# Feed-forward blocks of two groups, skewed accumulator drains and triangular diagonal scores in a gated-attention kernel

## The chip, the cores and the metric

The kernel runs on one core of one Trainium2 chip. The metric is the device time of one execution in microseconds; medians of several executions are given. The profiles show the TensorE clock granted in full (0.995 or more). A profile's span is 2 to 3 us shorter than the time of its execution. Names: PE is TensorE (matmuls), PEld its weight loads, DVE is VectorE, ACT is ScalarE, POOL is GpSimd, SP is SyncE, whose queue issues most DMAs here.

## The reference

```python
# u, v: (8, 3072, 256); z: (8, 3072, 64); w1, w2: (256, 1024); w_out: (1024, 256)
scores = (1 / S) * z @ z.T            # per batch, symmetric: 3072 x 3072
attn   = maximum(scores, 0) ** 2
x      = u * (attn @ v)               # 24576 rows of 256
out    = maximum(x @ w1, x @ w2) @ w_out
```

## The kernel before

A batch has 24 tiles of 128 rows, in 6 groups (512 query columns each), so there are 48 groups in all. For each group the kernel multiplies 24 tiles of attention by v (64-row matmuls, two at a time: rows 0 to 63 and 64 to 127 of the array work on their own halves of the contraction and sum into accumulators of their own). Since the attention matrix is symmetric, a block above the diagonal is computed once and its mirror image is made by a DMA transpose. Scores are computed up to 11 pairs of tiles ahead. After each group, the feed-forward of the group before it runs with 128-row matmuls, while ACT and DVE add up the two halves of the accumulators ("drain"). max(h1, h2) is computed as relu(x (w1 - w2)) + x w2, with w2 @ w_out folded once.

```python
def score_pair(b, g, m, ...):            # two tiles of scores; diagonal blocks in full
    for h in range(2):
        rows = ds(h * R, R)              # R = 64: one half of the array each
        nc.tensor.matmul(s_ps[h], zT[b][rows, 2 * m + h, :], zT[b][rows, ds(g * G, G), :]...)
    for h in range(2):
        nc.scalar.activation(r[:, h, :], s_ps[h], AF.Relu)
    nc.vector.tensor_mul(a[:, k : k + 2, :], r, r)
    ...                                  # mirror(b, g, blk): a DMA transpose on SP

def attn_unit(b, g, t, acc, first, last):
    for dc in range(KD):                 # two halves of d (128 columns each)
        for half in range(2):            # two halves of the array
            nc.tensor.matmul(acc[half][:, dc, :], v_sb[b][rows, t, ts(dc, P)], a..., ...)

def drain(acc):                          # both d halves at once, after the last tile
    for dc in range(KD):
        nc.scalar.copy(h, acc[1][:, dc, :])
    for dc in range(KD):
        nc.vector.tensor_add(hs[dc], hs[dc], acc[0][:, dc, :])

for i, (b, g) in enumerate(groups):
    for n in range(NT):                  # 24 tiles
        ahead(...)                       # at 8 of the tiles one more pair of scores
        attn_unit(b, g, n, acc, n == 0, n == NT - 1)
        if i and n == 12:
            waiting.append((*groups[i - 1], gate(*groups[i - 1], sums)))
        ...                              # loads, mirrors, z of the next batch in group 3
    now = waiting if i >= 2 else []      # one group per block (two at i = 2)
    g_sbs = [ff(w) for w in now[:1]]
    sums = drain(acc)
    ...                                  # ff2 of each; stores
```

## Time and profile before

The time before is 977.95 us (977.77 to 978.25). The page of the profiled execution gives for each engine the busy time, its share of the span and the number of instructions.

```profile
span 975.8 us, 19097 instructions
PE 962.4 (99%) x7994; PEld 516.8 (53%) x8042; DVE 495.4 (51%) x752; ACT 580.3 (59%) x1058; POOL 61.0 (6%) x118
PE 98%; DVE 1%; issue 0%; ACT 0%
```

The third line is the chain of work that ended last, by engine. PE is the bound in nearly the whole span. The view of the waits has for PE, the three largest first: engine, line and what it wanted, whom it waited for, then us in total, how often, and the longest.

```profile
PE acc_431 L184 <- DVE h_sb L195: 1.8, 1, 1.8
PE acc_644 L184 <- DVE h_sb L195: 1.8, 1, 1.8
PE s_ps L136 <- DVE r_sb L147: 1.5, 3, 0.7
```

These are the hand-overs of the accumulators after groups 0 and 1, where no feed-forward hides the drain, and waits for scores in the start; what is left out is 2.0 us in all, also of the start. The timeline of PE has the start, how long it took, the instruction and its count. Matmuls are pipelined, so what one costs is the time from its start to the next start.

```profile
202.21 0.38 PE L184 MATMUL acc_2591<-a_sb,v_sb 64*128 64x512 bf16 x1
202.22 0.38 PE L184 MATMUL acc_2592<-a_sb,v_sb 64*128 64x512 bf16 x1
202.43 0.38 PE L184 MATMUL acc_2591<-a_sb,v_sb 64*128 64x512 bf16 x1
202.43 0.38 PE L184 MATMUL acc_2592<-a_sb,v_sb 64*128 64x512 bf16 x1
202.74 3.63 PE L215 MATMUL d_ps<-xT,w_sb 128*128 128x512 bf16 x15
209.70 1.04 PE L244 MATMUL o_ps<-w_out_sb,g_sb 128*128 128x256 bf16 x8
210.67 0.39 PE L136 MATMUL s_ps<-zT 64*128 64x512 bf16 x2
210.90 0.38 PE L184 MATMUL acc_2859<-at_sb,v_sb 64*128 64x512 bf16 x1
```

A pair of 64-row matmuls takes 0.215 us (202.21 to 202.43). From the last such pair to the first 128-row matmul it is 0.31 us, so the switch costs 0.09 us; back again it costs the same.

| What | read from | value |
|---|---|---|
| pair of 64-row matmuls, 512 columns | timeline | 0.215 us |
| o_ps matmul, 256 columns | starts in the trace | 0.109 us |
| last attention pair to first d_ps | timeline | 0.31 us |
| last o_ps to first s_ps | starts in the trace | 0.205 us |
| feed-forward blocks | timeline | 46 |

### The profile page before, as it was taken

The page shows a single profiled execution, that of the slowest core. Times are in us where ns is not written, and L with a number is a line of the kernel's source. Part 1 is how long each engine was busy: PE and PEld are TensorE (multiplying, and loading weights), DVE is VectorE, ACT ScalarE, POOL GpSimd, SP SyncE. Part 2 cuts the span into 40 slices and gives each one's busy share as a digit, 9 for nine tenths or more (in the row PEclk, how much of TensorE's full clock was granted, in tenths as well). Part 3 has the DMA queues.
Part 4 walks back from the last instruction along what each step waited for, and adds up shares of the span by engine and source line. Part 5 has one row for each costly group of instructions (what it writes and reads, how often), then busy time and mean ns, then how long its engine had stood idle before and what let it go on. Part 6 is the DMA issues. An engine that isn't in the chain of part 4 may idle for free.

```text
span 975.8 us, 19097 instructions
## 1 busy us (share of the span) xinstructions
PE 962.4 (99%) x7994; PEld 516.8 (53%) x8042; DVE 495.4 (51%) x752; ACT 580.3 (59%) x1058; POOL 61.0 (6%) x118
## 2 busy tenths in 40 slices
PE   8899999999999999999999999999999999999998
PEld 3465555555555555555555555555555555555555
DVE  6645455554545544555445653555535564455523
ACT  7756466664666646666466664666546665466623
POOL 3101001000000000000000000000000000000000
PEclk9999999999999999999999999999999999999999
DMA  9999758786598866898668974789657896576411
GB/s 183 176 220 192 146 113 164 158 149 129 114 176 150 152 122 118 162 167 146 107 144 154 170 140 99 150 162 166 127 109 153 155 163 123 123 134 136 91 55 44
DMA packets 346005, 137.69 MB, mean 141 GB/s; under 512 B 324544, under 2 KB 325696, under 8 KB 345920
## 3 DMA queue, kind: packets, MB, share of 16 engines
q1 hardware_dynamic: 329504, 106.98, 54.9%
q0 software_dynamic: 16416, 29.50, 19.4%
q8 instruction: 63, 1.03, 0.4%
q14 instruction: 22, 0.18, 0.1%
HBM read 59.77 MB, written 25.17 MB: 87 GB/s over the span
## 4 chain that ended last, share of the span: by engine, by line
PE 98%; DVE 1%; issue 0%; ACT 0%
PE d_ps L215 17%; PE o_ps L244 17%; PE s_ps L136 8%; PE o_ps L236 4%; PE acc_12285 L184 1%; PE acc_12095 L184 1%; PE acc_10820 L184 1%; PE acc_10564 L184 1%; PE acc_10296 L184 1%; PE acc_10028 L184 1%; PE acc_9764 L184 1%; PE acc_9023 L184 1%; PE acc_8223 L184 1%; PE acc_7959 L184 1%; PE acc_1573 L184 1%; PE acc_11833 L184 1%
## 5 line engine op out<-in xcount | busy, mean ns | idle before, releaser
L151 ACT ACTIVATE r_sb<-s_ps 128x512 bf16<-128x512 f32 x663 | 360.4, 596 | 147.4 <-PE s_ps L136 147.3
L155 DVE TENSOR_TENSOR a_sb<-r_sb 128x1024 bf16<-128x1024 bf16 x335 | 231.5, 692 | 370.1 <-ACT r_sb L151 369.0
L184 PEld LDWEIGHTS <-v_sb 64*128 64x128 bf16 x4608 | 225.5, 94 | 270.7 <-issue 3.9
L244 PE MATMUL o_ps<-w_out_sb,g_sb 128*128 128x256 bf16 x1536 | 199.0, 273 | 0.0
L225 DVE TENSOR_SCALAR g_sb<-d_ps 128x512 bf16<-128x512 f32 x192 | 132.8, 692 | 95.9 <-PE d_ps L215 95.9
L223 ACT ACTIVATE g_sb<-d_ps 128x512 bf16<-128x512 f32 x192 | 114.6, 597 | 110.0 <-PE d_ps L215 109.9
L215 PE MATMUL d_ps<-xT,w_sb 128*128 128x512 bf16 x720 | 171.4, 380 | 2.5
L244 PEld LDWEIGHTS <-g_sb 128*128 128x128 bf16 x1536 | 150.2, 98 | 20.8
L251 ACT COPY o_sb<-o_ps 128x512 f32<-128x512 f32 x96 | 56.2, 585 | 129.1 <-PE o_ps L244 128.0
L136 PE MATMUL s_ps<-zT 64*128 64x512 bf16 x672 | 129.2, 377 | 2.3 <-DVE r_sb L147 1.5
L215 PEld LDWEIGHTS <-w_sb 128*128 128x128 bf16 x768 | 71.4, 98 | 98.5 <-issue 19.1
L113 POOL DMA_DIRECT2D un<-in_u_dram x48 | 25.6, 533 | 819.4 <-DMA uT<-un 798.2
L236 PE MATMUL o_ps<-W2o_sb,xT 128*128 128x256 bf16 x384 | 73.3, 273 | 0.0
L201 DVE SCALAR_TENSOR_TENSOR xT<-h_sb,uT 128x512 bf16<-128x512 f32 x96 | 61.7, 684 | 0.0
L136 PEld LDWEIGHTS <-zT 64*128 64x128 bf16 x672 | 33.1, 94 | 45.9 <-issue 10.0
L236 PEld LDWEIGHTS <-xT 128*128 128x128 bf16 x384 | 37.6, 98 | 14.1
L109 POOL DMA_DIRECT2D v_sb<-in_v_dram x48 | 25.9, 551 | 1.0 <-POOLq L426 0.8
L184 PE MATMUL acc_135<-a_sb,v_sb 64*128 64x512 bf16 x48 | 12.5, 376 | 0.0
L184 PE MATMUL acc_134<-a_sb,v_sb 64*128 64x512 bf16 x48 | 12.5, 376 | 0.0
L184 PE MATMUL acc_1795<-a_sb,v_sb 64*128 64x512 bf16 x48 | 11.6, 376 | 0.0
L184 PE MATMUL acc_3336<-a_sb,v_sb 64*128 64x512 bf16 x48 | 11.6, 376 | 0.0
L184 PE MATMUL acc_7960<-a_sb,v_sb 64*128 64x512 bf16 x48 | 11.6, 376 | 0.0
(302 smaller groups left out, 1213.5 us busy)
## 6 DMA issues: line engine op xcount, KB each, us to landing
out_dram<-o_sb SPq DMA_DIRECT2D x47, 512.0 KB, 3.0
v_sb<-in_v_dram POOLq DMA_DIRECT2D x48, 256.0 KB, 7.0
un<-in_u_dram POOLq DMA_DIRECT2D x48, 256.0 KB, 4.8
zn<-in_z_dram POOLq DMA_DIRECT2D x7, 384.0 KB, 6.2
at_sb<-a_sb SPq DMA_TRANSPOSE x120, 4.4
uT<-un SPq DMA_TRANSPOSE x48, 3.6
w_132<-in_moe_w_dram POOLq DMA_DIRECT2D x1, 512.0 KB, 5.2
w_131<-in_moe_w_dram POOLq DMA_DIRECT2D x1, 512.0 KB, 7.4
```

Source lines behind the costliest of these rows:

```text
L109: nc.gpsimd.dma_start(out=v_sb[b][:, sl, :], in_=by_tile(v[b])[:, sl, :])
L136: nc.tensor.matmul(s_ps[h], zT[b][rows, 2 * m + h, :], zT[b][rows, ds(g * G, G), :].rearrange("p t c -> p (t c)"), start=True, stop=True,)
L151: nc.scalar.activation(r[:, h, :], s_ps[h], AF.Relu)
L155: nc.vector.tensor_mul(a[:, k : k + 2, :], r, r)
L184: nc.tensor.matmul(o, v_sb[b][rows, t, ts(dc, P)], mv, start=first, stop=last)
L201: nc.vector.scalar_tensor_tensor(out=xT[:, dc, :].rearrange("p (t r) -> p t r", r=P), in0=hs[dc].rearrange("p (t r) -> p t r", r=P), scala ...
L215: nc.tensor.matmul(d_ps, w15_sb[:, kc, ts(nb, P)], xT[:, kc, :], start=(kc == 0), stop=(kc == KD - 1),)
L223: nc.scalar.activation(g_sb[:, nb, :], d_ps, AF.Relu)
L225: nc.vector.tensor_single_scalar(out=g_sb[:, nb, :], in_=d_ps, scalar=0.0, op=ALU.max)
L236: nc.tensor.matmul(o_ps[:, t, :], xT[:, dc, ts(t0 + t, P)], W2o_sb[:, dc, :], start=(dc == 0), stop=False,)
L244: nc.tensor.matmul(o_ps[:, t, :], g_sb[:, nb, ts(t0 + t, P)], w_out_sb[:, nb, :], start=False, stop=(nb == KF - 1),)
L251: nc.scalar.copy(o_sb[:, t0 : t0 + 2, :], o_ps)
```

## The change

The intent is to give PE fewer and shorter slots. (1) A feed-forward block follows every second group only and does two groups, so PE switches between 64-row and 128-row matmuls less often. (2) After the groups without a block the accumulators are handed over without a gap: in the last 9 tiles (4 in groups 0 and 1) the matmuls of the first d half all come before those of the second, and the next group begins the same way, so that one half drains while the other is computed; in groups 0 and 1 the drain is two plain copies, added later. (3) From batch 1 on, a diagonal block computes only its upper triangle, and three small DMA transposes fill in the rest; its tiles come last in the group. (4) The start has fewer score pairs ahead, and the prefetches in batch 0 are held back by a small DVE write before them.

```diff
+        triangle = blk == g and whole_first < (b, g)
+        lo = [(k + h) * P if triangle else 0 for h in range(2)]
         for h in range(2):
             rows = ds(h * R, R)
             nc.tensor.matmul(
-                s_ps[h],
+                s_ps[h][:, lo[h] :],
                 zT[b][rows, 2 * m + h, :],
-                zT[b][rows, ds(g * G, G), :].rearrange("p t c -> p (t c)"),
+                zT[b][rows, g * G + lo[h] // P : g * G + G, :].rearrange("p t c -> p (t c)"),
 ...
+        if triangle and m % 2 == 1:
+            for j in range(G - 1):
+                nc.sync.dma_start_transpose(
+                    a[:, j + 1 :, ts(j, P)], a[:, j, (j + 1) * P :]
+                )
 ...
+    def drain_fast(acc, dc):
+        hs = [hpool.tile([P, GW], fp32, name="h_sb") for half in range(2)]
+        nc.scalar.copy(hs[1], acc[1, dc])
+        nc.vector.tensor_copy(hs[0], acc[0, dc])
 ...
+    def ff_follows(i):
+        return i >= 2 and i % 2 == 0 or i == len(groups) - 1
+    def edge(i):
+        return 0 if ff_follows(i) else 4 if i < 2 else 9
+    def steps_of(i):
+        head = edge(i - 1) if i else 0
+        tail = NT - edge(i)
+        steps = [(n, dc) for dc in both for n in tiles[:head]]
+        steps += [(n, dc) for n in tiles[head:tail] for dc in both]
+        return steps + [(n, dc) for dc in both for n in tiles[tail:]]
+    def pair_slots(i):
 ...
+        if ff_follows(i):
+            return [3, 9, 15, 21, 26, 31, 36, 40]
+        return [0, 5, 10, 15, 20, 25, 30, 41]
 ...
+                if n == NT - 1 and not ff_follows(i):
+                    if i < 2:
+                        new[dc] = drain_fast(acc, dc)
+                    else:
+                        new.update(drain(acc, [dc]))
 ...
+                if i in (1, 2) and n == 10:
+                    for h in sums.values():
+                        nc.vector.tensor_add(h[0], h[0], h[1])
 ...
-            now = waiting if i >= 2 else []
+            now = waiting if ff_follows(i) else []
```

Cut from the diff: buffer counts (uT 4 to 3, h_sb 2 to 4, xT 3 to 4), the order of tiles, the triangular relus and squares, the held prefetches, the start.

More of the change, by code (lines that the diff above doesn't have):

```diff
@@ L49 @@
     unat = ctx.enter_context(tc.tile_pool(name="unat", bufs=2))
-    upool = ctx.enter_context(tc.tile_pool(name="upool", bufs=4))
+    upool = ctx.enter_context(tc.tile_pool(name="upool", bufs=3))
     apool = ctx.enter_context(tc.tile_pool(name="apool", bufs=11))
@@ L53 @@
     rpool = ctx.enter_context(tc.tile_pool(name="rpool", bufs=3))
-    hpool = ctx.enter_context(tc.tile_pool(name="hpool", bufs=2))
-    xpool = ctx.enter_context(tc.tile_pool(name="xpool", bufs=3))
+    hpool = ctx.enter_context(tc.tile_pool(name="hpool", bufs=4))
+    xpool = ctx.enter_context(tc.tile_pool(name="xpool", bufs=4))
     gpool = ctx.enter_context(tc.tile_pool(name="gpool", bufs=2))
@@ L65, with load_z @@
     zn, zd, zT, v_sb, un, uT = {}, {}, {}, {}, {}, {}
-    def load_z(b, lo, n):
+    def load_z(b, lo, n, held=False):
         if b not in zn:
@@ L72, in load_z @@
         sl = ds(lo, n)
+        if held:
+            nc.vector.memset(zn[b][:, lo, 0:1], 0.0)
         nc.gpsimd.dma_start(out=zn[b][:, sl, :], in_=by_tile(z[b])[:, sl, :])
@@ L103, in zT_pe, with load_v @@
         copy(zT[b][:, lo : lo + n, :], tp)
-    def load_v(b, lo, n):
+    def load_v(b, lo, n, held=False):
         if b not in v_sb:
@@ L108, in load_v @@
         sl = ds(lo, n)
+        if held:
+            nc.vector.memset(v_sb[b][:, lo, 0:1], 0.0)
         nc.gpsimd.dma_start(out=v_sb[b][:, sl, :], in_=by_tile(v[b])[:, sl, :])
@@ L124 @@
     later = []
+    whole_first = (0, NG - 1)
+    V_ORDER = (1, 2, 3, 4, 5, 0)
     V_LATE = [(3, 14), (4, 8), (4, 14), (5, 2), (5, 8), (5, 14)]
@@ L131, in score_pair @@
         a = A[b, g, blk]
+        k = 2 * (m % 2)
+        triangle = blk == g and whole_first < (b, g)
+        lo = [(k + h) * P if triangle else 0 for h in range(2)]
         s_ps = []
@@ L143, in score_pair @@
         r = rpool.tile([P, 2, GW], bf16, name="r_sb")
-        k = 2 * (m % 2)
         for h in range(2):
+            s, o = s_ps[h][:, lo[h] :], r[:, h, lo[h] :]
             if h == dve_half:
-                nc.vector.tensor_single_scalar(
-                    out=r[:, h, :], in_=s_ps[h], scalar=0.0, op=ALU.max
-                )
-            else:
-                nc.scalar.activation(r[:, h, :], s_ps[h], AF.Relu)
-            if halves:
-                nc.vector.tensor_mul(a[:, k + h, :], r[:, h, :], r[:, h, :])
-        if not halves:
-            nc.vector.tensor_mul(a[:, k : k + 2, :], r, r)
+                nc.vector.tensor_single_scalar(out=o, in_=s, scalar=0.0, op=ALU.max)
+            else:
+                nc.scalar.activation(o, s, AF.Relu)
+        if halves or triangle:
+            for h in range(2):
+                o = r[:, h, lo[h] :]
+                nc.vector.tensor_mul(a[:, k + h, lo[h] :], o, o)
+        else:
+            nc.vector.tensor_mul(a[:, k : k + 2, :], r, r)
+        if triangle and m % 2 == 1:
+            for j in range(G - 1):
+                nc.sync.dma_start_transpose(
+                    a[:, j + 1 :, ts(j, P)], a[:, j, (j + 1) * P :]
+                )
         if m % 2 == 1 and blk > g:
@@ L169, in mirror, with attn_unit, drain @@
         A[b, blk, g] = t
-    def attn_unit(b, g, t, acc, first, last):
+    def attn_unit(b, g, t, acc, dc, first, last):
         blk, j = divmod(t, G)
         a = A[b, g, blk]
-        for dc in range(KD):
-            for half in range(2):
-                rows = ds(half * R, R)
-                if blk >= g:
-                    o, mv = acc[half][:, dc, :], a[rows, j, :]
-                else:
-                    o = acc[half][:, dc, :].rearrange("p (k r) -> p k r", r=P)
-                    mv = a[rows, :, j, :]
-                nc.tensor.matmul(
-                    o, v_sb[b][rows, t, ts(dc, P)], mv, start=first, stop=last
-                )
-    def drain(acc):
-        hs = []
-        for dc in range(KD):
-            h = hpool.tile([P, GW], fp32, name="h_sb")
-            nc.scalar.copy(h, acc[1][:, dc, :])
-            hs.append(h)
-        for dc in range(KD):
-            nc.vector.tensor_add(hs[dc], hs[dc], acc[0][:, dc, :])
+        for half in range(2):
+            rows = ds(half * R, R)
+            if blk >= g:
+                o, mv = acc[half, dc], a[rows, j, :]
+            else:
+                o = acc[half, dc].rearrange("p (k r) -> p k r", r=P)
+                mv = a[rows, :, j, :]
+            nc.tensor.matmul(o, v_sb[b][rows, t, ts(dc, P)], mv, start=first, stop=last)
+    def drain(acc, dcs):
+        hs = {}
+        for dc in dcs:
+            hs[dc] = hpool.tile([P, GW], fp32, name="h_sb")
+            nc.scalar.copy(hs[dc], acc[1, dc])
+        for dc in dcs:
+            nc.vector.tensor_add(hs[dc], hs[dc], acc[0, dc])
+        return hs
+    def drain_fast(acc, dc):
+        hs = [hpool.tile([P, GW], fp32, name="h_sb") for half in range(2)]
+        nc.scalar.copy(hs[1], acc[1, dc])
+        nc.vector.tensor_copy(hs[0], acc[0, dc])
         return hs
@@ L260, with tiles_of @@
     W2o_sb = consts.tile([P, KD, D], bf16)
+    def ff_follows(i):
[3 more added lines that the diff above has]
+    def steps_of(i):
+        tiles, both = range(NT), range(KD)
+        head = edge(i - 1) if i else 0
[4 more added lines that the diff above has]
+    def pair_slots(i):
+        if i == 0:
+            return [1, 3] + list(range(6, 40, 4))
+        if i == 1:
+            return list(range(3, 41, 4))
+        if ff_follows(i):
+            return [3, 9, 15, 21, 26, 31, 36, 40]
+        return [0, 5, 10, 15, 20, 25, 30, 41]
     groups = [(b, g) for b in range(B) for g in range(NG)]
+    def tiles_of(b, g):
+        own = list(range(g * G, g * G + G))
+        rest = list(range(g * G + G, NT))
+        return list(range(g * G)) + (own + rest if (b, g) <= whole_first else rest + own)
     pairs, need = [], {}
     for i, (b, g) in enumerate(groups):
-        for n in range(NT):
-            if n // G >= g and n % 2 == 0:
-                pairs.append((b, g, n // 2))
-            need[i, n] = len(pairs)
+        order = [(b, g, m) for m in range(2 * g, NT // 2)]
+        base = len(pairs)
+        pairs += order
+        most = base
+        for n, t in enumerate(tiles_of(b, g)):
+            if t // G >= g:
+                most = max(most, base + order.index((b, g, t // 2)) + 1)
+            need[i, n] = most
     done = 0
@@ L278, in ahead @@
                 *pairs[done],
-                dve_half=1 if early and (done % 3 == 0 or done < 2) else None,
+                dve_half=1 if early and done % 3 == 0 else None,
                 halves=done == 0,
@@ L306, in new_acc @@
         def new_acc():
-            return [
-                acc_psum.tile([P, KD, GW], fp32, name=f"acc{half}") for half in range(2)
-            ]
+            return {
+                (half, dc): acc_psum.tile([P, GW], fp32, name=f"acc{half}{dc}")
+                for half in range(2)
+                for dc in range(KD)
+            }
         first_acc = new_acc()
@@ L315, in keep_warm @@
                 nc.tensor.matmul(
-                    first_acc[0][:, 0, :w], warm[:, :P], warm[:, :w], start=True, stop=True
+                    first_acc[0, 0][:, :w], warm[:, :P], warm[:, :w], start=True, stop=True
                 )
@@ L328 @@
         ahead(1)
-        zT_pe(0, 4, 8, "act")
+        zT_pe(0, 4, 8, "dve")
         keep_warm([P] * 2)
@@ L332 @@
         keep_warm([P] * 4)
-        ahead(3)
         waiting, sums = [], None
@@ L337 @@
             acc = new_acc() if i else first_acc
-            for n in range(NT):
+            new, slots = {}, pair_slots(i)
+            for slot, (n, dc) in enumerate(steps_of(i)):
                 k = need[i, n]
-                if b == 0 and g < 2:
-                    ahead(max(k, done + 1) if n % 2 == 0 and n < 22 else k)
-                else:
-                    more = n in (0, 3, 6, 9, 12, 15, 18, 20)
-                    ahead(max(k, min(done + 1, k + AHEAD)) if more else k)
-                if i == 0 and n == 5:
-                    zT_pe(0, 12, 8, "act")
-                if i == 0 and n == 11:
-                    zT_pe(0, 20, 4, "act")
-                attn_unit(b, g, n, acc, n == 0, n == NT - 1)
+                ahead(max(k, min(done + 1, k + AHEAD)) if slot in slots else k)
+                if i == 0 and slot in (10, 22):
+                    zT_pe(0, 12 if slot == 10 else 20, 8 if slot == 10 else 4, "act")
+                attn_unit(b, g, tiles_of(b, g)[n], acc, dc, n == 0, n == NT - 1)
+                if n == NT - 1 and not ff_follows(i):
+                    if i < 2:
+                        new[dc] = drain_fast(acc, dc)
+                    else:
+                        new.update(drain(acc, [dc]))
+                if dc:
+                    continue
+                if i in (1, 2) and n == 10:
+                    for h in sums.values():
+                        nc.vector.tensor_add(h[0], h[0], h[1])
+                    sums = {k: h[0] for k, h in sums.items()}
                 if i and n == 12:
@@ L367 @@
                 if later and n % 4 == 0 and (i > 1 or i == 1 and n > 12):
+                    later.sort(key=lambda block: block[2])
                     mirror(*later.pop(0))
@@ L379 @@
                     late = int(b == 0)
-                    if (g, n) == (2, 10):
-                        load_z(b + 1, 0, NT)
+                    if (g, n) == (2, 10 if b else 20):
+                        load_z(b + 1, 0, NT, held=late)
                     if (g, n) == (3, 4):
@@ L385 @@
                     if g >= 3 and n in (8, 14) and not late:
-                        load_v(b + 1, (2 * (g - 3) + (n == 14)) * G, G)
+                        load_v(b + 1, V_ORDER[2 * (g - 3) + (n == 14)] * G, G)
                     if late and (g, n) in V_LATE:
-                        load_v(1, V_LATE.index((g, n)) * G, G)
+                        load_v(1, V_ORDER[V_LATE.index((g, n))] * G, G, held=True)
             if i == 2:
@@ L400 @@
                     nc.scalar.copy(W2o_sb[:, dc, :], ps)
-            now = waiting if i >= 2 else []
+            now = waiting if ff_follows(i) else []
             g_sbs = [ff(w) for w in now[:1]]
-            sums = drain(acc)
+            sums = new or drain(acc, range(KD))
             for j, w in enumerate(now):
```

## The prediction

> **What bounds the kernel now.** TensorE. The page has PE busy 962.4 of 975.8 us (99%), ACT 59%, DVE 51%; the chain that ended last is 98% PE; the waits view gives PE only 7.1 us of waits: twice 1.78 us where the first two groups hand over their accumulators (waiting for the additions into h_sb), 2.3 us for scores and zT in the start. Only fewer or shorter PE slots help. A pair of 64-row matmuls of 512 columns takes a slot of 0.2155 us (timeline).
>
> **What the change removes.**
> 1. Switches between 64-row and 128-row matmuls. From the last attention start to the first d_ps is 0.31 us (202.43 to 202.74) instead of 0.215; from the last o_ps to the first s_ps about 0.20 instead of 0.11: 0.095 us each way. The Trainium skill ("TensorEngine Tiling (Array Packing)", Key Properties) says that changing the tiling mode drains the TensorE; this agrees. There are 46 feed-forward blocks now and 24 after: 22 x 0.19 = 4.2 us.
> 2. Triangles, 42 diagonal blocks in batches 1 to 7. Score pairs shrink from 512+512 to 512+384 and 256+128 columns. The halves run side by side and start in order, so the longer counts: only the second pair gains half a slot (0.107 us): 4.5 us, say 4.2.
> 3. The two hand-overs of 1.78 us. The copies of one d half run on ACT and DVE together (0.6 us each), but four tiles hide only 0.9 us and DVE still has a square (0.69 us) in front: I expect 0.6 us left at each, 2.3 us saved.
> 4. The start: attention no longer waits for a third and fourth score pair: 0.4 us.
>
> **What it adds.**
> - At the 22 odd boundaries without a feed-forward the accumulators must drain under the other d half. From the trace: last matmul's start to end of drain is 0.41 + 0.6 (copy) + 0.67 (addition), about 1.75 us; nine tiles and a score pair give 2.37 us. No wait expected.
> - Scores run less far ahead. By my count of slots, in group 2 of each batch the last pair is computed 13 slots (2.8 us) before use, where score to square takes 2.25 us: just free. In batch 0 it is 9 to 12 slots (was 15 to 21), while DVE gets the delayed additions and the gating (1.3 us each): 1.5 us of new waits.
> - 126 small DMA transposes, a tenth more transposed blocks, on a queue with a 55% share, some 13 us before use: no effect.
>
> **Sum.** 4.2 + 4.2 + 2.3 + 0.4 - 1.5 = 9.6, about 10 us, 1.0%, all on the critical path.
>
> Predicted 968.0 us; eight times in ten between 963.5 and 972.5. Faster by over 2%: 0.02; within 2%: 0.95; slower by over 2%: 0.03.
>
> **What would show each step.** Timeline: feed-forward blocks of two groups, none after odd groups; s_ps pairs of 256 and 128 columns with 0.107 us to the next start. Waits: the two 1.78 us down to about 0.6; nothing at odd boundaries; no PE wait for a triangle's DMA; 1 to 2 us for a_sb in the first 60 us.
>
> **What would make it wrong.** PE waits at odd boundaries (0.3 us each would cost 7 us) because ACT or DVE drains late; a stall in group 2 of every batch for scores (1 us each: 7 us); the 384-column half saving too (2 us more); transposes landing late in batch 0, whose DMA is busiest.

## The result, and the profile after

The changed kernel takes 969.06 us (968.62 to 969.40, 4 runs) against 977.95 us; the ratio is 0.9908 (0.9891 to 0.9926). Ratios are the mean time of one kernel's runs over that of the other's of the same rounds, so not quite the ratio of the medians.

The lines of the page that answer to those of before:

```profile
span 966.4 us, 19478 instructions
PE 954.8 (99%) x7994; PEld 621.6 (64%) x8042; DVE 487.2 (50%) x847; ACT 557.6 (58%) x1058; POOL 61.0 (6%) x118
PE 96%; DVE 1%; issue 1%; ACT 1%; DMA 1%; DVEq 0%; POOLq 0%
```

PE is as full as before, with the same number of matmuls, in 9.4 us less. The largest of its waits (the first is the start's first memset, as before):

```profile
PE acc_134 L374 <- DVE warm L351: 1.2, 1, 1.2
PE acc_427 L199 <- DVE a_sb L166: 1.1, 3, 0.5
PE acc_427 L199 <- DVE h_sb L214: 0.5, 1, 0.5
PE s_ps L147 <- DVE r_sb L158: 0.5, 1, 0.5
PE acc_134 L199 <- DMA v_sb<-in_v_dram: 0.4, 1, 0.4
PE acc_637 L199 <- DVE a_sb L166: 0.4, 1, 0.4
```

The two hand-overs of 1.78 us have become one of 0.5. All these waits lie in the first 51 us: acc_427 is group 1, acc_637 group 2. No boundary after that has a wait for a drain. In exchange, PE now waits 1.5 us in groups 1 and 2 for squares of scores (a_sb) that DVE does late; waits for relus (r_sb) there were before too (1.5 us, now 0.5).

A count in the trace, from the start of the last o_ps of one block to the start of the first d_ps of the next, shows the steady state of a batch (batches 2 to 6, the same in every one; the rows one_ff, full_mm and swap_rows are experiments below). With one group per block the stretches are those of groups 0 to 5; with two, those of groups 1 and 2, 3 and 4, and 5 and the next batch's 0:

```
attention between blocks, us            sum   feed-forward blocks, us
before    12.40 12.40 12.40 12.40 12.18 11.32   73.10   6 x  7.72
one_ff    12.29 12.29 12.29 12.18 12.07 11.32   72.44   6 x  7.72
full_mm   24.48       24.48       23.19         72.15   3 x 15.54
after     24.37       24.16       23.08         71.61   3 x 15.54
swap_rows 24.32       24.00       23.03         71.35   3 x 15.54
```

The start of the first block (in the third group) came at 53.79 us instead of 55.17. These 1.4 us are not all gain: a count in the trace gives 31 pairs of score matmuls before that block where there were 33, and the two missing ones (0.43 us) are only done later. So 1.0 us of the gain lies in the start. The profile also shows something that I had not expected. PE's timeline after the change, around a triangle:

```profile
200.61 0.38 PE L199 MATMUL acc_2833<-at_sb,v_sb 64*128 64x512 bf16 x1
200.67 0.38 PE L199 MATMUL acc_2835<-at_sb,v_sb 64*128 64x512 bf16 x1
200.83 0.38 PE L199 MATMUL acc_2833<-at_sb,v_sb 64*128 64x512 bf16 x1
200.89 0.22 PE L147 MATMUL s_ps<-zT 64*128 64x128 bf16 x1
200.94 0.38 PE L199 MATMUL acc_2835<-at_sb,v_sb 64*128 64x512 bf16 x1
201.05 0.27 PE L147 MATMUL s_ps<-zT 64*128 64x256 bf16 x1
201.16 0.38 PE L199 MATMUL acc_2833<-at_sb,v_sb 64*128 64x512 bf16 x1
```

acc_2833 is summed by rows 0 to 63, acc_2835 by rows 64 to 127. In the program the 256-column matmul (rows 0 to 63) stands before the 128-column one (rows 64 to 127), and yet the latter starts 0.16 us earlier, and even the attention matmul behind it (200.94) is ahead. The two halves of the array run as two streams, and the second has got ahead by the columns that it was spared. What becomes of this lead shows at the end of the stretch, where the first d_ps of the next block begins:

```profile
211.74 0.38 PE L199 MATMUL acc_2836<-a_sb,v_sb 64*128 64x512 bf16 x1
211.84 0.38 PE L199 MATMUL acc_2833<-a_sb,v_sb 64*128 64x512 bf16 x1
212.06 0.38 PE L199 MATMUL acc_2834<-a_sb,v_sb 64*128 64x512 bf16 x1
212.36 0.39 PE L234 MATMUL d_ps<-xT,w_sb 128*128 128x512 bf16 x1
```

Rows 64 to 127 start their last matmul at 211.74 (acc_2836). Rows 0 to 63 still have two to do (211.84 and 212.06), and the block starts 0.31 us after the last of these, as it did before the change. After the block both halves start level again (228.34). The lead has bought nothing.

### The profile page after: what moved, and what is told of

The parts are those of the page before. It is cut to its first block, busy times and chain, and to the rows that moved or that the text cites. A ratio compares the mean times of both kernels' runs of the same rounds, so it can differ in the third digit from the quotient of the medians.

```text
span 966.4 us, 19478 instructions
## 1 busy us (share of the span) xinstructions
PE 954.8 (99%) x7994; PEld 621.6 (64%) x8042; DVE 487.2 (50%) x847; ACT 557.6 (58%) x1058; POOL 61.0 (6%) x118
## 4 chain that ended last, share of the span: by engine, by line
PE 96%; DVE 1%; issue 1%; ACT 1%; DMA 1%; DVEq 0%; POOLq 0%
PE o_ps L263 17%; PE d_ps L234 17%; PE s_ps L147 7%; PE o_ps L255 4%; DMA v_sb<-in_v_dram 1%; DVE a_sb L166 1%; PE acc_12604 L199 1%; PE acc_6354 L199 1%; PE acc_4771 L199 1%; PE acc_3187 L199 1%; PE acc_11103 L199 1%; PE acc_9519 L199 1%; PE acc_7936 L199 1%; PE acc_1582 L199 1%; PE acc_1581 L199 1%
## 5 line engine op out<-in xcount | busy, mean ns | idle before, releaser
L199 PEld LDWEIGHTS <-v_sb 64*128 64x128 bf16 x4608 | 314.6, 94 | 181.4 <-issue 5.9
L160 ACT ACTIVATE r_sb<-s_ps 128x512 bf16<-128x512 f32 (+3 forms) x664 | 333.8, 555 | 90.4 <-PE s_ps L147 88.8
L166 DVE TENSOR_TENSOR a_sb<-r_sb 128x1024 bf16<-128x1024 bf16 x251 | 173.6, 692 | 243.0 <-ACT r_sb L160 239.0
L234 PE MATMUL d_ps<-xT,w_sb 128*128 128x512 bf16 x720 | 167.4, 379 | 2.6 <-issue 0.2
L147 PE MATMUL s_ps<-zT 64*128 64x512 bf16 (+3 forms) x672 | 148.6, 357 | 0.9 <-DVE r_sb L158 0.5
L147 PEld LDWEIGHTS <-zT 64*128 64x128 bf16 x672 | 47.6, 94 | 29.0 <-issue 4.6
L164 DVE TENSOR_TENSOR a_sb<-r_sb 128x512 bf16<-128x512 bf16 (+3 forms) x170 | 47.9, 323 | 14.7 <-ACT r_sb L160 14.5
L199 PE MATMUL acc_134<-a_sb,v_sb 64*128 64x512 bf16 x24 | 8.7, 377 | 0.5 <-DMA v_sb<-in_v_dram 0.4
L199 PE MATMUL acc_136<-a_sb,v_sb 64*128 64x512 bf16 x24 | 8.7, 378 | 0.0
L199 PE MATMUL acc_137<-a_sb,v_sb 64*128 64x512 bf16 x24 | 8.5, 376 | 0.0
L199 PE MATMUL acc_135<-a_sb,v_sb 64*128 64x512 bf16 x24 | 8.5, 376 | 0.0
```

Source lines behind the costliest of these rows:

```text
L147: nc.tensor.matmul(s_ps[h][:, lo[h] :], zT[b][rows, 2 * m + h, :], zT[b][rows, g * G + lo[h] // P : g * G + G, :].rearrange("p t c -> p (t ...
L160: nc.scalar.activation(o, s, AF.Relu)
L164: nc.vector.tensor_mul(a[:, k + h, lo[h] :], o, o)
L199: nc.tensor.matmul(o, v_sb[b][rows, t, ts(dc, P)], mv, start=first, stop=last)
L234: nc.tensor.matmul(d_ps, w15_sb[:, kc, ts(nb, P)], xT[:, kc, :], start=(kc == 0), stop=(kc == KD - 1),)
```

## The experiments

Each kernel is the changed one with the edit shown. Those of one batch ran on the same chip, with the kernel before (978.0 us in each batch). The changed kernel itself ran only in the first batch (again, one_ff, full_mm, swap_rows); the others ran on another chip and are compared with its 968.96 us, as the kernel before took the same time on both.

### What the two main parts are worth

> The changed kernel unedited, so that the others of this batch have it beside them on the same chip: 969 us, PE waits of about 5 us in all, none of them at a boundary after the third group.

It took 968.96 us (968.32 to 969.18), and its trace had one wait that the first trace had not: 0.6 us for the transposed z of a batch. More of that below.

```diff
 def ff_follows(i):
-    return i >= 2 and i % 2 == 0 or i == len(groups) - 1
+    return i >= 2
```

> The changed kernel with a feed-forward block after every group again (46 blocks instead of 24, and no boundary without one). If the pair-wise blocks gain only by 22 fewer switches each way between 64-row and 128-row matmuls, at 0.19 us for both, the time rises by 4.1 us to 973.2. Rival: pairing the groups gains (or costs) something else, such as ACT and DVE evictions that no longer stand in the way of the drains; then the rise is not 4 us, and PE waits at the boundaries change.

It took 972.78 us (972.60 to 973.20), 3.8 us more than the changed kernel, and PE had no wait at any boundary after the second group. The switches account for it (22 x 0.188 = 4.1 by the gaps between starts; the changed kernel also loses 0.6 us that one_ff does not, see full_mm, so that without this loss the rise would be 4.4). The rival, that pairing gains through other engines, is not needed. The edit also removes the skew at these boundaries and moves their score pairs, since both follow ff_follows; PE has no wait there in either kernel.

```diff
             nc.tensor.matmul(
-                s_ps[h][:, lo[h] :],
+                s_ps[h],
                 zT[b][rows, 2 * m + h, :],
-                zT[b][rows, g * G + lo[h] // P : g * G + G, :]...
+                zT[b][rows, g * G : g * G + G, :]...
```

> The changed kernel with the diagonal blocks' score matmuls at all 512 columns again; the relus, the squares and the small transposes stay triangular. If the triangle gains through TensorE's slots alone, the time rises by 42 x 0.107 = 4.5 us to 973.5. Rival: it gains through less work on ACT and DVE; then the time stays at 969.

It took 972.70 us (971.80 to 972.97), 3.7 us more than the changed kernel, though ACT and DVE still did triangles: the gain is PE's slots. It is 0.8 us less than 42 x 0.107. The table says where: the stretches are 0.11, 0.32 and 0.11 us shorter than with full matmuls, which is five times 0.107 per batch and not six. The sixth is lost in group 2 of each batch. The timeline of the changed kernel there, first DVE, then PE:

```profile
286.04 1.28 DVE L220 SCALAR_TENSOR_TENSOR xT<-h_sb,uT 128x512 bf16<-128x512 f32 x2
287.25 0.68 DVE L166 TENSOR_TENSOR a_sb<-r_sb 128x1024 bf16<-128x1024 bf16 x1
287.63 0.42 PE L147 MATMUL s_ps<-zT 64*128 64x128 bf16 x2
287.98 0.37 PE L199 MATMUL acc_3863<-a_sb,v_sb 64*128 64x512 bf16 x1
```

DVE's gating (the multiplication by u, 1.28 us) stands before the square; the square ends at 287.93, and the attention matmul that needs it starts at 287.98. The 256-column slot in front of it lasted 0.198 us instead of 0.107, in this spot of each of the 7 batches, 0.6 us in all. So the supply of scores in group 2, which I had counted as "just free", is late by 0.1 us once the slots are shorter. That the gating is the cause is read from the order of times (ACT had finished the relus of this square at 286.70, DVE the gating at 287.33); I did not run a kernel with the gating moved. The trace of one_ff has no such slot: there all six triangles count (73.10 - 72.44 = 0.66 us per batch). The loss needs pairing and triangles together, and so both 3.8 and 3.7 us are what is left after it; each part alone is worth about 0.6 us more.

### Can the lead of one half be used?

```diff
         for h in range(2):
-            rows = ds(h * R, R)
+            rows = ds((1 - h if triangle and m % 2 else h) * R, R)
```

> The changed kernel, but in the second pair of a triangle the 256-column half runs on rows 64 to 127 and the 128-column half on rows 0 to 63, so each half of the array has 640 columns per diagonal block instead of 768 and 512. If the two halves run as independent streams that may drift apart (in the trace of the changed kernel a 128-column matmul of the one half starts before the 256-column one issued ahead of it), the lead of the first pair is used up: 42 x 0.053 = 2.2 us less, 966.8. If they start strictly in the order of the program, as I predicted with, the longer matmul of each pair counts and nothing changes: 969.

It took 967.01 us (966.44 to 967.86; ratio to before 0.9887), 1.95 us less than the changed kernel. The table has 0.16 us for each of five triangles per batch, where it was 0.107: each half now has 640 columns per triangle (512 + 128 and 384 + 256), and what one half gains in the first pair is given to the other in the second. Five triangles of 0.053 us more in 7 batches are 1.9 us, as measured. The halves do run as independent streams, and a lead is worth something only if the other half catches up before the next switch to 128 rows: in this trace both halves start their last matmul before the block at the same time (212.52 and 212.53). This is the fastest kernel, and its only edit is which rows two matmuls use.

### The boundaries without a block

```diff
 def edge(i):
-    return 0 if ff_follows(i) else 4 if i < 2 else 9
+    return 0 if ff_follows(i) else 4
```

> The changed kernel with 4 instead of 9 tiles skewed at the 22 odd boundaries. If a boundary is free only where the 1.75 us from the last matmul's start to the end of its drain fit under the matmuls of the other d half, 4 tiles (1.08 us) are too few: at least 0.7 us of PE wait for h_sb at each, about 1.1 us where the score pair in the tail keeps ACT busy first: 984 to 994. If the skew hardly matters (rival: a plain hand-over would do), under 972.

It took 992.32 us (991.41 to 993.04), 23 us more. PE's waits:

```profile
PE acc L199 <- DVE h_sb L207: 18.5, 22, 1.0
```

There are 22 waits, one at each such boundary, 0.84 us on average, between the 0.7 us that the count of 1.75 against 1.08 gives and the 1.1 us with ACT's score pair on top. One wait of 1.9 us for the transposed z of a batch comes on top; of that kind more below. Without enough skew the pairing would lose far more than its 3.8 us.

```diff
-        return [0, 5, 10, 15, 20, 25, 30, 41]
+        return [0, 5, 10, 15, 20, 25, 30, 38]
```

> The changed kernel with 9 tiles skewed, but the last score pair of an odd group issued just before the last matmuls of the first d half (slot 38) instead of in the second half (slot 41). ACT then does its two relus (1.1 us) before the drain's copy, and by my count the accumulators are free 2.7 us after the last matmul's start, where 2.15 us are covered: 0.55 us of wait at each of 22 boundaries, 12 us in all: 981. If where the pair stands makes no difference to the boundary: 969.

It took 985.95 us (981.35 to 988.43), 17 us more and with a spread that the others have not. The waits are of two kinds:

```profile
PE s_ps L147 <- DMA zT<-zd: 8.4, 3, 5.1
PE acc L199 <- DVE h_sb L207: 5.0, 15, 0.3
```

The boundary waits are there, at 15 of the 22 boundaries and 0.33 us each rather than the 0.55 at each that I had counted. The larger part is a wait for the DMA that transposes z of the next batch. I had expected nothing of the kind, and looked for it in all traces: how long before its first score pair does that transpose land?

```
margin of zT, us, for batches 2 to 7 (batch 1: 6 to 14 in all of these)
before   7.23  6.42  7.44  8.16  7.88  6.93
one_ff   6.50 10.05  9.35  8.31  8.43  7.10
after    1.36  2.53  2.49  0.77  1.70  0.10
again    1.61  0.05  2.07  1.55  2.28  0.05      (0.05: the pair starts as it lands)
slot38   0.05  0.05  0.19  0.05  0.09  0.05
```

So the change has used up nearly all of a margin of 6 to 8 us. z is doubled by DVE and transposed in group 3 of the batch before; the next batch's first scores follow early in group 4, and the feed-forward block that used to lie between the two (for batch 2 from 202.7 to 210.5 us) is now elsewhere. With one group per block (one_ff, which has the triangles too) the margin is as large as before.

```diff
 # with the edit of slot38:
-                    if (g, n) == (3, 4):
+                    if (g, n) == (3, 4) and b == 0:
                         double_z(b + 1, 0, NT); zT_dma(b + 1)
 ...
                 ff2(*w, g_sbs[j])
+                if j == 0 and g == 2 and 0 < b < B - 1:
+                    double_z(b + 1, 0, NT); zT_dma(b + 1)
```

> The kernel with the late score pair at slot 38 (985.95 us, 5.0 us of PE waits for h_sb in its trace and 8.4 us for the transposed z of the next batch) with one thing more: from batch 1 on, z of the next batch is doubled and transposed inside the feed-forward block after group 2, not in group 3. If the waits for zT are a second cause, of their own, they go and the time falls by 8 to 11 us, to 975 to 978, with the 5 us for h_sb left. If the boundary alone is slow, it stays at 985.

It took 978.57 us (976.12 to 983.09), 7.4 us less than without the early z, a little above the range I gave. The waits:

```profile
PE acc L199 <- DVE h_sb L207: 5.0, 15, 0.3
PE s_ps L147 <- DMA zT<-zd: 1.8, 2, 1.1
```

The boundary wait is unchanged to the tenth, and the wait for zT has fallen from 8.4 to 1.8: they are two causes. It has not gone, because SP takes its DMAs in order: from batch 2 on the early transpose stood 5 to 8 us in its queue and then took 4 to 12 us to issue.

> The changed kernel with z of the next batch doubled and transposed inside the feed-forward block after group 2. In the trace of the changed kernel it lands 0.1 to 2.5 us before its first score pair needs it (6 to 8 us in the kernel before). If that margin is a risk only, the margin grows past 10 us and the time stays within 0.5 us of 969 with less spread; if it costs something unseen, it falls by more.

The same early z without the edit of slot38 took 968.65 us (968.42 to 969.34): the margin became 5.0 to 7.3 us, not the 10 I had hoped for, and the time is that of the changed kernel within the noise. In the changed kernel, then, the thin margin is a risk of half a microsecond now and then (0.6 us once in two traces) and not a steady cost.

### Other parts of the change

```diff
-                        load_z(b + 1, 0, NT, held=late)        # and held=True for v
+                        load_z(b + 1, 0, NT, held=False)       # and False for v; z at tile 10
```

> The changed kernel without the held prefetches in batch 0: the loads of z and v of batch 1 are issued as soon as the queue comes to them, z ten tiles earlier. If they only keep DMA out of the way and PE never waits for it there: 969, the same PE waits. Rival: they let the mirrored blocks and weights of batch 0 land in time; then new PE waits for a DMA before 60 us, 1 to 3 us more.

It took 968.43 us (968.24 to 968.60), with the same waits of PE but for the first tile of v (0.8 us; 0.4 in the changed kernel, and between 0.2 and 1.5 in the other traces): holding the prefetches back does nothing measurable here.

```diff
-                        nc.vector.tensor_add(h[0], h[0], h[1])
+                        (nc.gpsimd if i == 1 else nc.vector).tensor_add(h[0], h[0], h[1])
```

> The changed kernel with the two additions of the drained halves of group 0 done by POOL instead of DVE, in group 1, where PE waits 2.4 us longer than a slot for squares and relus of scores that DVE does late. If DVE's backlog is the cause, taking 1.3 us of additions off it saves 0.7 to 1.3 us: 968. If POOL is slow or disturbs DVE: 969 or more.

It took 969.89 us (968.91 to 971.37), no gain and perhaps a loss. The timeline of POOL, DVE and PE in group 1 shows why:

```profile
24.76 2.49 POOL L412 TENSOR_TENSOR h_sb<-h_sb 128x512 f32<-128x512 f32 x2
25.06 3.34 DVE L166 TENSOR_TENSOR a_sb<-r_sb 128x1024 bf16<-128x1024 bf16 x2 [1.63 <-ACT r_sb L160]
27.86 0.82 PE L199 MATMUL acc<-a_sb,v_sb 64*128 64x512 bf16 x6 [1.55 <-DVE a_sb L166]
```

Two squares, 0.69 us each elsewhere, took DVE 3.34 us: the first began at 25.06 while POOL was adding and ended at 27.80, POOL's two additions (1.27 us each) were done at 27.25, and only at 27.86 did the matmul that needs the square start, after a wait of 1.55 us. The Trainium skill ("SBUF — State Buffer", "SBUF: two separate sides") says that DVE and GpSimd share a pair of ports, which a DVE instruction with two inputs in SBUF and a GpSimd one that reads SBUF each hold until their end, the other waiting in full; this trace agrees, in one place measured once: the square ended only after both additions. The work left DVE's list but not its time.

### Longer blocks

```diff
 # with the early z:
-    return i >= 2 and i % 2 == 0 or i == len(groups) - 1
+    return i % 3 == 2
```

> The same with feed-forward blocks of three groups (16 blocks instead of 24). By 0.19 us for a pair of switches: 1.5 us less, 967.4. If longer blocks bring new waits (scores, mirrored blocks or stores late), more than 969.

It took 978.15 us (974.96 to 981.81), nearly 11 us more than I expected. PE, ACT and SP, from the views of the waits and the timelines of ACT and of SP's queue:

```profile
PE s_ps L147 <- ACT o_sb L270: 8.9, 4, 3.9
193.65 1.07 ACT L270 COPY o_sb<-o_ps 128x512 f32<-128x512 f32 x2 [8.83 <-DMA out_dram<-o_sb]
165.11 15.77 SPq L181 DMA_TRANSPOSE at_sb<-a_sb  x3
180.98 4.31 SPq L169 DMA_TRANSPOSE a_sb<-a_sb  x3
185.39 1.26 SPq L122 DMA_TRANSPOSE uT<-un  x1
186.74 1.82 SPq L181 DMA_TRANSPOSE at_sb<-a_sb  x1
188.65 1.03 SPq L274 DMA_DIRECT2D out_dram<-o_sb  x1
```

The block's first result was in o_sb by 174 us (ACT's second copy starts at 173.38). Its store was issued at 188.65, because SP was still issuing transposes that stand before it in the queue. o_sb has two buffers, so ACT could not copy the third group's result, the PSUM buffers stayed full, and PE waited for scores. In this place the queue was behind before the early zT came to be issued (189.77), so it was not the early z that delayed this store; but three groups without the early z were not run, and how much of the loss it has elsewhere stays open.

> Three groups per block, early z, and the second pair of a triangle with its halves swapped over the rows of the array: 1.5 us less by switches and 2 us less by the swap (as measured alone): 965.4, one per cent and a quarter under the kernel before.

The combination of three groups, early z and swapped rows took 978.24 us in the median of its four fast runs (973.37 to 983.85; two more took 989.78 and 990.18): the same wait (10.6 us for o_sb in its trace) and a wide spread. It is no improvement; swap_rows is.

The reason that SP is behind can be read from its issues. The triangles' transposes are small, but each holds SP's queue. The lines are the triangles' and the mirrored blocks' transposes after the change, and the mirrored blocks' before it:

```profile
L169 SPq DMA_TRANSPOSE a_sb<-a_sb x126: 1170/1200/2746, 91.8 to 915.9; - x126
L181 SPq DMA_TRANSPOSE at_sb<-a_sb x120: 1678/2190/7981, 11.4 to 909.1; - x120
L165 SPq DMA_TRANSPOSE at_sb<-a_sb x120: 1315/1918/9177, 10.9 to 917.2; - x120
```

The numbers after the count are the shortest, median and longest time in ns that one issue took. A transpose of 1 to 3 blocks of 128 by 128 takes 1.2 us to issue, one of 16 blocks 2.2 us (1.9 before). Summed over the trace, SP spends this long issuing DMAs: 397 us before, 613 in one_ff, 636 after, 766 in three_zt. The first step is the triangles (168 us of it); the rest is mostly the same 120 mirrored blocks taking longer to issue (264 us in all before, 348 after). Why they do was not tested.

## Why the prediction was right

Predicted 968.0, measured 969.06; the gain was put at about 10 us and is 8.9. The two large terms were right in mechanism and size. What the prediction did not have is the loss in group 2, and that the sum is still so near is in part luck, as the point on the start shows. Point by point:

- **Switches: 4.2 predicted, 3.8 measured** (one_ff), 4.4 without the loss in group 2. Right in mechanism and size.
- **Triangles: 4.2 predicted, 3.7 measured** (full_mm), 4.3 without the loss in group 2. The count of the longer half was right as a sum and wrong in its reason: I had the halves "start in order", and they do not. Each half is a stream; rows 0 to 63 have the longer matmul in both pairs and so set the time, and the lead of the other half is thrown away at the next switch. swap_rows, 1.95 us faster, shows it. What I had listed under "what would make it wrong", the 384-column half saving too, was there to be had, but not in this change.
- **Hand-overs and start: 2.3 + 0.4 saved and 1.5 lost, so 1.2 predicted; 1.4 measured** (the start of the first block), of which 0.43 us are the two score pairs put off and 1.0 us is gain. Near by luck, since the parts differ: the hand-overs kept one wait of 0.54 us, not two of 0.6, and saved about 3.0 us by the gaps between starts; attention began 0.75 us earlier (between 6.8 and 8.2 us in the traces of the changed start, as the first tile of v happened to land), but the 0.4 us for the third and fourth score pair are that postponed work and no saving; the late squares of groups 1 and 2 cost about 2.1 us by the same count of gaps.
- **Odd boundaries free: right.** No wait in the trace, and edge4 and slot38 show that they are free only by the nine tiles and by where the last score pair stands.
- **Group 2 of each batch "just free": wrong by a little.** It is 0.1 us late per batch and takes back one triangle of six, 0.6 us in all. The prediction had no term for it.
- **126 transposes: "no effect".** True of the time, for the wrong reason: I looked at the share of the DMA engines (55%), while what they fill is the time SP takes to issue them. The change left SP busy issuing for 66% of the span, from 41% (636 of 966 and 397 of 976 us), and, with the pairing, brought the margin of z's transpose from 6 to 8 us down to 0.1 to 2.5. It costs almost nothing until the next change: slot38, three_zt and best all ran into DMAs issued or landed late.

The three measured parts add up, 3.8 + 3.7 + 1.4 = 8.9 us, to the difference of the medians (977.95 - 969.06), but that is a coincidence: the first two count the loss of group 2 twice, and the third counts 0.4 us of postponed work as gain. Counted once each, 4.4 + 4.3 - 0.6 + 1.0 = 9.1 us, against 8.9 by the medians and 9.4 by the spans of the two traces.

## What to carry to other kernels

When PE is 99% busy, count its slots by shape and mode from start to start: here the switch of tile shape (0.19 us there and back) and the columns of each half of the array gave each of the two large terms to 0.2 us. When two halves of the array work on matmuls of unequal length, balance the columns per half over the stretch between two switches, not per pair. When parts of a change are switched off one at a time, look in the traces for a loss that two of them share, before adding up. And after a change that costs nothing, ask what margin it used: read how long before its use each DMA lands and how full the issuing queue is, for the next change will pay for it.

## What the Trainium skill lacked or had wrong

- "TensorE: Matmul & The Clock Gate", Part 3, The mechanism, says that matmuls start and end strictly in the order of the program. Ends are only modelled in these traces, but for the starts it does not hold: in this trace a 128-column matmul on rows 64 to 127 started 0.16 us before the 256-column one on rows 0 to 63 that stands before it, and swap_rows gained 1.95 us because the halves may drift apart. "TensorEngine Tiling (Array Packing)", Key Properties, says that tiles operate independently, which is what the runs show.
- "TensorEngine Tiling (Array Packing)", Key Properties, says that a change of tiling mode drains TensorE, without a number: here 0.09 us each way by the gaps between starts, and 3.8 us (4.4 without the loss in group 2) for 22 switches there and back.
- "DMA: Bandwidth & Descriptors", DMA Transpose (X-bar), has no time for how long a transpose within SBUF holds the queue that issues it, and the one figure elsewhere on the page, in a table on a later chip, is given for "previous generations" and not for this chip by name: here 1.2 us for 1 to 3 blocks of 128 by 128 and 2.2 us (median; up to 8.0) for 16.
